# Banded attention rebuilt with float32 operands and a fixed instruction order, ahead of a two-stage feed-forward network

## The chip, the cores and the metric

The kernel runs on one core of a Trainium2 chip. The metric is device time in microseconds (us); lower is better. One profiled execution of the kernel before gives the rows below; its time stands beside its span in the table. PE is the matrix engine (PEld its weight loads), DVE the vector engine, ACT the scalar engine, POOL the general engine GpSimd, SP the engine that issues most transfers.

## The reference

```python
scores = scale * np.matmul(q, k.transpose(0, 1, 3, 2))      # q, k, v: (2, 8, 768, 64)
keep = is_sink | in_window                                  # first 4 positions, or 0 <= rel < 128
a = softmax(np.where(keep, scores, -1e9))
x = np.matmul(a, v)  ->  (1536, 512)
h = x @ w_in;  g = max(h, 0) + log1p(exp(-abs(h)));  x = g @ w_out       # 512 -> 2048 -> 512
h = x @ w_in2; g = h * clip(h + 3, 0, 6) / 6;        out = g @ w_out2    # the same sizes
```

All is float32, with a window of 128 and 4 sinks.

## The kernel before

Sequence positions are cut in groups of 128: `NG` = 12 groups, 6 for each of 2 batch elements. A group of 8 heads is handled as two half groups ("quads") of 4 heads, counted by `n` = 0 to 23 in the main loop of `banded_attention`. A query group needs the keys of its own group and of the one before, and 16 columns for sinks, so a score row has 272 columns (128 in the first group of a batch element, where `i` = 0; sinks are used where `i` > 1).

Every product is made to float32 accuracy out of cheaper ones. Queries and keys are split into a high and a low float32r half by ACT and POOL (L395 to L407), and a score is three matrix products of halves (L456; a head has 64 rows, so the heads of a pair take the two row halves of the array). DVE scales, masks and takes the maximum (L460), ACT takes the exponential (L465), PE transposes the probabilities (L492; the sink columns, gathered by POOL, in L500). ACT and DVE write them out of PSUM as two float16 halves (L475, L478). The values are cut by POOL into three bfloat16 parts (L427, L428), and probabilities times values is five products for each head and block (L533), with three more for the sinks (L517). Then DVE divides by the sum (L541 to L544), PE turns the result (L553), and ACT and DVE store it as two halves of `xT` (L556, L557).

The feed-forward part (`Ffn`) works on blocks of 512 tokens: three blocks of the first network, then three of the second, 16 chunks each; a chunk has 12 products for `h` (L111) and 12 for `y` (L163), 2304 in all. Its weights arrive as 8-byte numbers and each half chunk is converted on the way (`Weights.half`: three DVE steps, L70 to L76, one of ACT, L80, one of POOL, L81). Six such halves are called for inside the attention loop. PE, DVE, ACT and POOL each work through one stream in order; the scheduler of the building program sets that order from the order of the code and its own estimates.

Of the kernel before, what the change touches and what calls it, by code (L numbers as in the profile page):

```python
# [10 lines left out]
F16 = mybir.dt.float16  # L11
# [8 lines left out]
P = 128  # L20
NEG = 1.0e9
PSCALE = 4096.0
# [4 lines left out]
TB = 2  # L27

# [64 lines left out]
class Ffn:  # L93
# [91 lines left out]
    def run(self, specs, out, nblk, w0, pool2):  # L185
# [15 lines left out]
        for s in range(n + 2):  # L201
# [22 lines left out]
def sink_window_attention_ffn_kernel(  # L224
# [46 lines left out]
    with ExitStack() as body:  # L271
# [14 lines left out]
        w.upto(2 * NW0)  # L286
# [4 lines left out]
        for c in range(NW0, 16):  # L291
            for io in range(2):
                w.add("w1", c, io, w1_in, w1_out, wpool1)
        w.fetch()
        ffn.run(specs, out, NT // 512, 2 * NW0, lambda c: wpool0 if c < NW0 else wpool1)
# [3 lines left out]
    with tc.If(rv < 1):  # L299
        nc.scalar.preload_act_table_set("natural_log_exp_and_others")  # L300
        with ExitStack() as body:
# [13 lines left out]
            ffn.run(specs, out, NT // 512, 4, lambda c: wpool)  # L315


def banded_attention(ctx, tc, qT_d, kT_d, v, ident, NSv, Wv, xT, psa, isq, w):
    nc = tc.nc
# [3 lines left out]
    NP = H // 2  # L323

# [6 lines left out]
    st = {}  # L331

    def fetch(g):
        b, i = divmod(g, NB)
        s = st.setdefault(g, {})
        for nm, src in (("q", qT_d), ("k", kT_d)):
            t = two.tile([P, NP, P], F32, tag="n" + nm, bufs=2, name=f"n{nm}_{g}")
            nc.sync.dma_start(t, src[b].rearrange("(p t) d s -> (t d) p s", t=2)[:, :, i * P : (i + 1) * P])
            s["n" + nm] = t
        t = thr.tile([P, H, D], F32, tag="nv", name=f"nv_{g}")  # L340
        nc.sync.dma_start(t, v[b, i * P : (i + 1) * P])
        s["nv"] = t

    def fetch_sinks(b):
        s = st[b * NB]

        t = two.tile([P, H, D], F32, tag="vs", name=f"vs_{b}")
        nc.gpsimd.memset(t, 0.0)
        for r in range(8):
            nc.sync.dma_start(t[r * MAXSINK : (r + 1) * MAXSINK, r % 4 :: 4, :], v[b, 0:MAXSINK, r % 4 :: 4, :])  # L350
        s["nvs"] = t

    fetch(0)


    hid = -NEG / isq
    rmc = one.tile([P, P], F32, name="rmc")
    nc.gpsimd.iota(rmc, pattern=[[-1, P]], base=0, channel_multiplier=1, allow_small_or_imprecise_dtypes=True)
    col = one.tile([P, P], F32, name="col")
    nc.gpsimd.iota(col, pattern=[[1, P]], base=0, channel_multiplier=0, allow_small_or_imprecise_dtypes=True)  # L360
    wm = one.tile([P, 1], F32, name="wm")
    nc.vector.tensor_scalar(out=wm, in0=Wv, scalar1=-float(P), scalar2=None, op0=ALU.add)
# [13 lines left out]
    nc.vector.tensor_tensor(out=m_zero, in0=mB, in1=mS, op=ALU.mult)  # L376
    nc.vector.tensor_tensor(out=m_one[:, 0, 0:P], in0=mA, in1=mS, op=ALU.mult)
    nc.vector.tensor_copy(m_one[:, 1, 0:P], mB)
    nc.vector.memset(m_one[:, :, P:SLOTW], hid)
    nc.vector.tensor_copy(m_odd[:, 0, 0:P], mA)  # L380
    nc.vector.tensor_copy(m_odd[:, 1, 0:P], mB)
    nc.vector.tensor_copy(m_even[:, 0, 0:P], mB)
    nc.vector.tensor_copy(m_even[:, 1, 0:P], mA)
    for m in (m_odd, m_even):
        for j in range(2):
            nc.vector.tensor_scalar(
                out=m[:, j, P:SLOTW], in0=mS[:, j * SK : (j + 1) * SK], scalar1=hid, scalar2=None, op0=ALU.mult
            )

    ring = one.tile([P, 2, NP, 4, SLOTW], F32R, name="ring")  # L390

    def load_q(g):
        s = st[g]
        qT = two.tile([P, 2, NP, P], F32R, tag="qT", bufs=2, name=f"qT_{g}")
        nc.scalar.activation(qT[:, 0], s["nq"], AF.Copy)  # L395
        eng = nc.gpsimd if g else nc.vector
        eng.tensor_tensor(out=qT[:, 1], in0=s["nq"], in1=qT[:, 0].bitcast(F32), op=ALU.subtract)
        s["qT"] = qT

    def load_k(g):  # L400
        b, i = divmod(g, NB)
        s = st[g]
        pos = SLOTPOS[g % 4]
        hi, lo = ring[:, 0, :, pos, 0:P], ring[:, 1, :, pos, 0:P]
        nc.scalar.activation(hi, s["nk"], AF.Copy)  # L405
        eng = nc.gpsimd if g else nc.vector
        eng.tensor_tensor(out=lo, in0=s["nk"], in1=hi.bitcast(F32), op=ALU.subtract)  # L407
        if i == 0:
            ks = two.tile([P, 2, NP, MAXSINK], F32, tag="ks", name=f"ks_{b}")
            for a in range(2):  # L410
                nc.gpsimd.tensor_copy(ks[:, a], ring[:, a, :, pos, 0:MAXSINK].bitcast(F32))
            st["ks", b] = ks
        if i < 4:
            ks = st["ks", b]
            for a in range(2):
                nc.gpsimd.tensor_copy(ring[:, a, :, pos, P:SLOTW], ks[:, a, :, (i % 2) * SK : (i % 2 + 1) * SK])

    def top(x):
        return x.bitcast(BF16).rearrange("p (n t) -> p n t", t=2)[:, :, 1]

    def values(g, src="nv", dst="V", pool=thr):

        s = st[g]
        x = s[src].rearrange("p h d -> p (h d)")
        res = pool.tile([P, H * D], F32, tag=dst + "r", name=f"{dst}r_{g}")
        v3 = pool.tile([P, H * D], BF16, tag=dst + "3", name=f"{dst}3_{g}")
        nc.gpsimd.tensor_tensor(out=res, in0=x, in1=top(x), op=ALU.subtract)  # L427
        nc.gpsimd.tensor_tensor(out=v3, in0=res, in1=top(res), op=ALU.subtract)  # L428
        s[dst] = (top(x), top(res), v3)

    def scores(g, quad):
        b, i = divmod(g, NB)
# [4 lines left out]
        pt = two.tile([P, 4, 2, SLOTW], F32, tag="P", bufs=2, name=f"P_{g}_{quad}")  # L437
        s["P", quad] = pt
        if i == 0:
            mask = m_zero  # L440
            n = P
        else:
            ee, oo = sorted((SLOTPOS[(g - 1) % 4], SLOTPOS[g % 4]))
            mask = (m_one if i == 1 else m_odd if i % 2 else m_even).rearrange("p a c -> p (a c)")
            n = 2 * SLOTW
        for p in range(quad * 2, quad * 2 + 2):

            pss = [psa.tile([P, 512], F32, tag="s", name=f"s_{g}_{p}_{t}")[:, 0:n] for t in range(2)]
            for m, (a, c) in enumerate(((0, 0), (0, 1), (1, 0))):
                for t in range(2):  # L450
                    rows = slice(t * D, (t + 1) * D)
                    if i == 0:
                        rhs = ring[rows, c, p, SLOTPOS[g % 4], 0:P]
                    else:
                        rhs = ring[rows, c, p, ee : oo + 1 : oo - ee, :]
                    nc.tensor.matmul(pss[t], s["qT"][rows, a, p, :], rhs, start=(m == 0), stop=(m == 2))  # L456
            for t in range(2):
                h = 2 * p + t
                xs = thr.tile([P, 2 * SLOTW], F32, tag="xs", bufs=4, name=f"xs_{g}_{h}")[:, 0:n]
                st["ttr"] = nc.vector.tensor_tensor_reduce(  # L460
                    out=xs, in0=pss[t], in1=mask, scale=-isq, scalar=3.0e38,
                    op0=ALU.add, op1=ALU.min, accum_out=s["mx"][:, h : h + 1],
                )
                dst = pt[:, h - quad * 4].rearrange("p a c -> p (a c)")[:, 0:n]
                nc.scalar.activation(  # L465
                    dst, xs, AF.Exp, scale=-1.0, bias=s["mx"][:, h : h + 1], accum_out=s["sum"][:, h : h + 1]
                )

        if i > 1:
            s["PS", quad] = two.tile([P, 2, 4, 2, SK], F32, tag="PS", name=f"PS_{g}_{quad}")  # L470
            for a in range(2):
                nc.gpsimd.tensor_copy(s["PS", quad][:, a], pt[:, :, :, P:SLOTW])

    def evac_hi(t, ps):
        nc.scalar.activation(t, ps, AF.Copy, scale=PSCALE)  # L475

# [228 lines left out]
```

## Time and profile before

| | |
|---|---|
| median of 3 runs | 670.83 us (670.52 to 672.7) |
| the profiled execution | 670.09 us, span 668.2 us |
| busy: PE, DVE, ACT, POOL | 644.7, 364.2, 358.4, 274.9 us |
| mean granted clock of PE | 0.996 |
| attention alone on PE | to 129.3 us of the span, its rest mixed with L111 until 145.8 us |

The span runs from the first to the last instruction. A busy PE is not a PE at its peak, since the ends of pipelined products are modelled; starts of neighbouring rows tell its pace.

### The profile page before, as it was taken

The numbers are of one execution on the slowest core, as the hardware profiler recorded it, in microseconds if no ns is written. First come the engines' busy times: TensorE is split into PE (matmuls) and PEld (weight loads), VectorE is DVE, ScalarE is ACT, GpSimd is POOL, SyncE is SP. The second block draws the span as 40 slices with busy tenths as digits, with TensorE's granted clock in tenths as the row PEclk, the third lists the DMA queues.
The fourth block names the chain that finished last, engine by engine and source line by source line (L and its number), as shares of the span: only waits on it lengthen the run. The fifth ranks groups of instructions, "written<-read, shape, count | busy, mean of one in ns | idle before, by whom it ended". The sixth has DMA issues, their size and how long they took to land.

```text
span 668.2 us, 10211 instructions
## 1 busy us (share of the span) xinstructions
PE 644.7 (96%) x3760; PEld 527.3 (79%) x3760; DVE 364.2 (54%) x730; ACT 358.4 (54%) x755; POOL 274.9 (41%) x272
## 2 busy tenths in 40 slices
PE   1999999999999999999999999999999999999996
PEld 0777877887878888888888888888888888888884
DVE  6468899979998233222689899422232222322222
ACT  2668888786878766566867874322222222222221
POOL 6446756468898545444589894100000000000000
PEclk9999999998999999999999999999999999999999
DMA  6832321289100000001465652000010000100001
GB/s 173 271 92 74 113 64 34 87 275 372 41 1 0 1 0 1 0 1 32 153 196 190 209 164 66 2 0 1 0 64 0 1 1 0 64 0 1 1 0 68
DMA packets 38746, 47.01 MB, mean 70 GB/s; under 512 B 2848, under 2 KB 31520, under 8 KB 38688
## 3 DMA queue, kind: packets, MB, share of 16 engines
q1 hardware_dynamic: 38400, 46.28, 21.6%
q8 instruction: 31, 0.51, 0.3%
q14 instruction: 27, 0.22, 0.1%
q10 hardware_dynamic: 288, 0.00, 0.0%
HBM read 43.12 MB, written 3.15 MB: 69 GB/s over the span
## 4 chain that ended last, share of the span: by engine, by line
PE 89%; DVE 3%; ACT 3%; POOL 2%; issue 2%; DMA 1%; SPq 0%; POOLq 0%; ACTq 0%; DVEq 0%
PE y_w L163 37%; PE h_w L111 36%; PE s L456 6%; PE pt L492 4%; PE o L533 4%; DMA nk<-in_k_dram 1%; PE o L517 1%; POOL w_w L81 1%; PE xtr L553 1%; POOL u_w L132 1%; POOL g_w L138 1%; DVE PT L478 0%; ACT P L465 0%; ACT e_w L129 0%; ACT u_w L130 0%
## 5 line engine op out<-in xcount | busy, mean ns | idle before, releaser
L111 PE MATMUL h_w<-xT,w_w 128*128 128x512 f32 x1152 | 282.4, 391 | 1.8 <-POOL w_w L81 1.3
L111 PEld LDWEIGHTS h_w<-xT,w_w 128*128 128x128 f32 x1152 | 216.4, 188 | 47.7 <-POOL w_w L81 1.7
L163 PE MATMUL y_w<-g_w,w_w 128*128 128x512 f32 x576 | 142.2, 390 | 0.1
L163 PE MATMUL y_w<-w_w,g_w 128*128 128x512 f32 x576 | 138.9, 389 | 0.0
L163 PEld LDWEIGHTS y_w<-g_w,w_w 128*128 128x128 f32 x576 | 108.4, 189 | 23.3 <-POOL g_w L138 0.8
L163 PEld LDWEIGHTS y_w<-w_w,g_w 128*128 128x128 f32 x576 | 107.9, 188 | 23.2 <-ACT g_w L143 0.4
L81 POOL TENSOR_TENSOR w_w<-t_w,w_w 128x512 fp32r<-128x512 f32 x64 | 83.9, 1312 | 33.9 <-ACT w_w L80 33.5
L142 DVE SCALAR_TENSOR_TENSOR h_w<-e_w,h_w 128x512 f32<-128x512 f32 x48 | 33.4, 696 | 89.0 <-ACT e_w L140 89.0
L140 ACT ACTIVATE e_w<-h_w 128x512 f32<-128x512 f32 x48 | 28.7, 599 | 96.2 <-PE h_w L111 94.6
L144 DVE SCALAR_TENSOR_TENSOR g_w<-h_w,g_w 128x512 fp32r<-128x512 f32 x48 | 33.2, 691 | 83.6 <-ACT g_w L143 83.6
L143 ACT ACTIVATE g_w<-h_w 128x512 fp32r<-128x512 f32 x48 | 28.7, 598 | 91.0 <-PE y_w L163 90.7
L132 POOL TENSOR_TENSOR u_w<-u_w,e_w 128x512 f32<-128x512 f32 x48 | 62.2, 1295 | 36.4 <-ACT u_w L131 34.4
L138 POOL TENSOR_TENSOR g_w<-e_w,g_w 128x512 fp32r<-128x512 f32 x48 | 62.2, 1296 | 32.8 <-ACT g_w L137 32.6
L456 PE MATMUL s<-ring,qT 64*128 64x272 f32 (+1 forms) x288 | 47.7, 344 | 14.9 <-ACT ring L405 7.6
L135 DVE SCALAR_TENSOR_TENSOR h_w<-h_w,r_w 128x512 f32<-128x512 f32 x48 | 33.4, 696 | 51.8 <-ACT r_w L133 51.8
L465 ACT ACTIVATE P<-xs,mx 128x272 f32<-128x272 f32 (+1 forms) x96 | 47.3, 496 | 15.4 <-DVE mx L460 15.2
L456 PEld LDWEIGHTS s<-ring,qT 64*128 64x128 f32 x288 | 33.9, 212 | 23.2 <-DVE mx L460 8.8
L136 DVE TENSOR_TENSOR e_w<-h_w,u_w 128x512 f32<-128x512 f32 x48 | 33.0, 688 | 28.6 <-POOL u_w L132 28.4
L80 ACT ACTIVATE w_w<-t_w 128x512 fp32r<-128x512 f32 x64 | 40.0, 625 | 13.1 <-DVE t_w L76 12.8
L128 ACT ACTIVATE e_w<-h_w 128x512 f32<-128x512 f32 x48 | 28.4, 592 | 32.6 <-PE h_w L111 23.3
L137 ACT ACTIVATE g_w<-e_w 128x512 fp32r<-128x512 f32 x48 | 30.0, 624 | 28.1 <-DVE e_w L136 19.5
L70 DVE TENSOR_SCALAR m_w<-raw_w 128x512 int32<-128x512 int32 x56 | 38.8, 693 | 8.3 <-DMA raw_w<-in_moe_w_in_dram 3.8
(89 smaller groups left out, 717.1 us busy)
## 6 DMA issues: line engine op xcount, KB each, us to landing
raw_w<-in_moe_w_in_dram SPq DMA_DIRECT2D x32, 512.0 KB, 4.8
raw_w<-in_moe_w_out_dram SPq DMA_DIRECT2D x32, 512.0 KB, 4.5
nq<-in_q_dram SPq DMA_DIRECT2D x12, 256.0 KB, 3.0
nk<-in_k_dram SPq DMA_DIRECT2D x12, 256.0 KB, 3.7
nv<-in_v_dram SPq DMA_DIRECT2D x12, 256.0 KB, 2.9
out_dram<-o SPq DMA_DIRECT2D x12, 256.0 KB, 2.1
vs<-in_v_dram SPq DMA_DIRECT2D x16, 8.0 KB, 3.4
words<-in_n_sink_dram ACTq DMA_DIRECT2D x1, 1.0 KB, 4.0
```

Source lines behind the costliest of these rows:

```text
L70: nc.vector.tensor_scalar(out=m, in0=hi, scalar1=3, scalar2=0x3FFFFFF8, op0=ALU.logical_shift_left, op1=ALU.bitwise_and)
L80: nc.scalar.activation(wt[:, 0, :], t.bitcast(F32), AF.Copy)
L81: nc.gpsimd.tensor_tensor(out=wt[:, 1, :], in0=t.bitcast(F32), in1=wt[:, 0, :].bitcast(F32), op=ALU.subtract)
L111: nc.tensor.matmul(h, wt[:, ws, kk * P : (kk + 1) * P], xT[:, xs, kk, t0 : t0 + 512], start=(n == 0), stop=(n == 11),)
L132: nc.gpsimd.tensor_tensor(out=u, in0=u, in1=e, op=ALU.subtract)
L135: nc.vector.scalar_tensor_tensor(out=h, in0=h, scalar=0.0, in1=r, op0=ALU.max, op1=ALU.add)
L138: nc.gpsimd.tensor_tensor(out=glo, in0=e, in1=ghi.bitcast(F32), op=ALU.subtract)
L142: nc.vector.scalar_tensor_tensor(out=h, in0=e, scalar=6.0, in1=h, op0=ALU.min, op1=ALU.mult)
L144: nc.vector.scalar_tensor_tensor(out=glo, in0=h, scalar=1.0 / 6.0, in1=ghi.bitcast(F32), op0=ALU.mult, op1=ALU.subtract)
L163: ins = nc.tensor.matmul(y, lhsT, rhs, start=(c == 0 and n == 0), stop=(c == 15 and n == 2))
L456: nc.tensor.matmul(pss[t], s["qT"][rows, a, p, :], rhs, start=(m == 0), stop=(m == 2))
L465: nc.scalar.activation(dst, xs, AF.Exp, scale=-1.0, bias=s["mx"][:, h : h + 1], accum_out=s["sum"][:, h : h + 1])
```

## The change

The attention is written anew. The splits are gone: scores (L457 of the changed kernel), transposes (L499) and probabilities times values (L541, sinks L526) take float32 operands as they are. A score is one product instead of three, a head and block one instead of five. Two copies of 512 columns take the transposed probabilities out of PSUM, one by ACT (L514), one by DVE (L512). There are four score banks instead of three. Keys go by DMA straight into the ring, `fetch` runs three groups ahead instead of two, and the first group's transfers are cut in two and shared between SP and ACT. Masks are made one by one, just before the half group that needs them. 22 products of zeros stand at the start of PE's stream, and 6 in each of the first three rounds. Everything inside `in_order` keeps the order of the code on each engine. Five weight halves are converted inside the attention instead of six (and two behind it), and the first network's weights are listed in another order.

```diff
+HALVES = (5, 9, 13, 17, 21)
+WARM = 22
...
-    nc.scalar.dma_start(words[:, 1, :], window.bitcast(I32).partition_broadcast(P))
+    nc.sync.dma_start(words[:, 1, :], window.bitcast(I32).partition_broadcast(P))
...
+        order = [(0, 0)] + [x for c in range(15) for x in ((c + 1, 0), (c, 1))] + [(15, 1)]
...
-        w.upto(2 * NW0)
...
-        ffn.run(specs, out, NT // 512, 2 * NW0, lambda c: wpool0 if c < NW0 else wpool1)
+        ffn.run(specs, out, NT // 512, w.done, lambda c, io: homes[c, io])
...
-            for m, (a, c) in enumerate(((0, 0), (0, 1), (1, 0))):
-                for t in range(2):
-                    nc.tensor.matmul(pss[t], s["qT"][rows, a, p, :], rhs, start=(m == 0), stop=(m == 2))
+                nc.tensor.matmul(ps, s["q"][rows, p, :], rhs, start=True, stop=True)
...
-            evac_hi(t[:, 0], ps)
-            evac_lo(t[:, 1], ps, t[:, 0])
+        if m == 1:
+            nc.vector.tensor_copy(t, ps)
+        else:
+            nc.scalar.activation(t, ps, AF.Copy)
...
+            for k, (o, gg) in enumerate(blocks):
                 nc.tensor.matmul(
-                    s["o"][:, h, :], lh, rh, start=(i <= 1 and m == 0),
-                    stop=(m == len(terms) - 1 and (i <= 1 or hh == 3)),
+                    s["o"][:, h, :], t[:, o : o + P], st[gg]["v"][:, h, :], start=(k == 0 and (i <= 1 or hh == 0)),
+                    stop=(k == len(blocks) - 1 and i <= 1),
                 )
...
+    def keep_busy(n):
+
+        for _ in range(n):
+            nc.tensor.matmul(spare, z[:, 0:P], z, start=True, stop=True)
+
+    with in_order(tc):
+        fetch(0)
...
+        keep_busy(WARM)
+        masks(0)
+        fetch(1)
+        fetch_sinks(0)
+        fetch(2)
+        keep_sinks(0)
+        for n in range(NQ + 3):
...
+            if new:
+                scores(n)
+            if done is not None:
+                normalise(done)
+            if n < 3:
+                keep_busy(6)
+            if old:
+                transposes(n - 1, 1)
+                transposes(n - 1, 2)
+            if new:
+                exps(n, 0)
+            if n >= 4 and n % 2 == 0:
+                store_lo(n // 2 - 2)
+            if old:
+                copies(n - 1, 1)
+                copies(n - 1, 2)
+                apply_v(n - 1, 0)
+            if new:
+                exps(n, 1)
+                transposes(n, 0)
+            if done is not None:
+                turn_x(done)
+            if old:
+                apply_v(n - 1, 1)
+                apply_v(n - 1, 2)
+                if n % 2 == 0:
+                    inverse((n - 1) // 2)
+            if new:
+                copies(n, 0)
+            if done is not None:
+                store_hi(done)
...
+            if n < 3:
+                masks(n + 1)
+            if n in HALVES:
                 w.half()
```

DVE at the start, in the kernel before: from the first mask step to the first score step (`xs`); `mA` to `m_zero` are masks of 128 rows and 128 columns.

```order
L368 TENSOR_SCALAR mB<-rmc,val 128x128
L371 TENSOR_SCALAR mS<-col,val 128x128
...
L377 TENSOR_TENSOR m_one<-mA,mS 128x128
L380 COPY m_odd<-mA 128x128
L383 COPY m_even<-mA 128x128
L376 TENSOR_TENSOR m_zero<-mB,mS 128x128
L378 COPY m_one<-mB 128x128
L381 COPY m_odd<-mB 128x128
L382 COPY m_even<-mB 128x128
L386 TENSOR_SCALAR m_even<-mS 128x8
L460 ISA xs_0_177,mx_167<-s_0_0_169,m_zero 128x128
```

The same place now:

```order
L409 TENSOR_SCALAR mB<-rmc,val 128x128
L291 TENSOR_TENSOR fl<-fl 128x1
L410 TENSOR_TENSOR mB<-mB,tB 128x128
L293 TENSOR_TENSOR near<-fl 128x1
L411 TENSOR_SCALAR mS<-col,val 128x128
L412 TENSOR_TENSOR m_zero<-mB,mS 128x128
L469 ISA xs_0_197,mx_181<-s_0_183,m_zero 128x128
```

Four mask steps stand ahead of the first score step now; those of `m_one`, `m_even` and `m_odd` have moved behind the score steps of half groups 0, 1 and 2.

PE in the middle of the attention, in the kernel before (group 5, second half; `pt` and `pts` are transposes, `o` the attention's result, of which only the first of 40 pieces stands here):

```order
L456 MATMUL s_2_0_1196<-ring,qT_919 128x272 x3
L492 MATMUL pt_1_0_1120<-ident,P_1_973 128x128 x4
L492 MATMUL pt_1_1_1128<-ident,P_1_973 128x128 x4
L500 MATMUL pts_1_1136<-ident,PS_1_1002 128x128
L456 MATMUL s_2_1_1197<-ring,qT_919 128x272 x3
L456 MATMUL s_3_0_1210<-ring,qT_919 128x272 x3
L517 LDWEIGHTS PTS_0_1023
L517 MATMUL o_1144<-vs_245,PTS_0_1023 128x256
...
L533 MATMUL o_1144<-nv_578,PT_0_0_1010 128x64
```

One whole round of the loop now (`n` = 8, group 4, first half):

```order
L457 MATMUL s_0_631<-ring,q_376 128x272
...
L457 MATMUL s_3_637<-ring,q_376 128x272
L499 MATMUL pt_1_639<-ident,P_562 128x128 x4
L490 MATMUL pts_644<-ident,PS_601 64x128
L541 MATMUL o_590<-v_173,PT_0_618 128x64
...
L541 MATMUL o_590<-v_255,PT_0_618 128x64
L499 MATMUL pt_0_669<-ident,P_630 128x128 x4
L541 MATMUL o_590<-v_173,PT_1_653 128x64
...
L541 MATMUL o_590<-v_255,PT_1_653 128x64
L526 MATMUL o_590<-vs_170,PTS_655 128x256
```

The four heads' scores stand together with their row halves alternating, and between them and the transposes that need them lies work of the half group before; `o` has 8 products and one for the sinks.

## Rows read from the trace of the kernel before

**Rows 1.** Windows: each engine's busy time and instructions, PE's granted clock, DMA, GB/s.
```profile
16.70:41.80 25.10, 25.10 (x156) 19.47 (x156) 12.10 (x49) 15.73 (x51) 11.98 (x12) 1.00 0.71 226
41.80:129.30 87.50, 86.31 (x1192) 69.09 (x1190) 79.59 (x252) 74.95 (x230) 51.92 (x78) 1.00 0.22 62
145.80:232.00 86.20, 84.30 (x362) 68.21 (x361) 67.69 (x103) 64.56 (x116) 69.77 (x55) 0.98 0.27 93
```

**Rows 2.** Timeline of PE: start, length, instructions merged, and the releaser.
```profile
16.69 1.54 PE L456 MATMUL s<-ring,qT 64*128 64x128 f32 x9 [7.25 <-DVE mx L460]
...
28.26 1.12 PE L492 MATMUL pt<-ident,P 128*128 128x128 f32 x4
...
39.54 1.05 PE L456 MATMUL s<-ring,qT 64*128 64x272 f32 x3
...
41.80 0.84 PE L553 MATMUL xtr<-ident,x 128*128 128x128 f32 x4
...
69.99 0.65 PE L456 MATMUL s<-ring,qT 64*128 64x272 f32 x6
...
71.11 0.20 PE L533 MATMUL o<-nv,PT 128*128 128x64 bf16 x1
...
72.27 0.19 PE L533 MATMUL o<-Vr,PT 128*128 128x64 bf16 x1
...
72.86 0.64 PE L456 MATMUL s<-ring,qT 64*128 64x272 f32 x3
73.43 0.66 PE L492 MATMUL pt<-ident,P 128*128 128x128 f32 x4
...
129.33 4.80 PE L111 MATMUL h_w<-xT,w_w 128*128 128x512 f32 x20
...
145.76 5.71 PE L163 MATMUL y_w<-g_w,w_w 128*128 128x512 f32 x24
```

**Rows 3.** Timeline of DVE at the start.
```profile
8.44 1.02 DVE L368 TENSOR_SCALAR mB<-rmc,val 128x128 f32<-128x128 f32 x1
...
9.87 0.29 DVE L370 TENSOR_TENSOR mB<-mB,tB 128x128 f32<-128x128 f32 x1
...
12.55 1.28 DVE L380 COPY m_odd<-mA 128x128 f32<-128x128 f32 x1
...
16.35 0.28 DVE L460 CUSTOM_DVE_ANT_0 xs<-s,m_zero 128x128 f32<-128x128 f32 x1
```

**Rows 4.** The chain that ended last: start, length, what.
```profile
1.24 5.66 DMA nk<-in_k_dram
...
651.25 2.72 PE h_w L111 x12
...
662.73 0.69 DVE o L182
```

**Rows 5.** Groups by line: count, busy us, mean ns of one, idle before.
```profile
L456 PEld LDWEIGHTS s<-ring,qT 64*128 64x128 f32 x288 | 33.9, 212 | 23.2 <-DVE mx L460 8.8 <-ACT ring L405 7.6 <-issue 3.6
...
L73 DVE SCALAR_TENSOR_TENSOR m_w<-raw_w,m_w 128x512 int32<-128x512 int32 x56 | 38.8, 692 | 1.2
...
L460 DVE CUSTOM_DVE_ANT_0 xs<-s,m_odd 128x272 f32<-128x272 f32 x32 | 13.2, 431 | 1.4 <-PE s L456 1.3
...
L460 DVE DVE_READ_ACCUMULATOR2_ANT mx<- 128x1 f32 x96 | 7.9, 82 | 0.0
...
L553 PEld LDWEIGHTS xtr<-ident,x 128*128 128x128 f32 x48 | 5.4, 146 | 0.1
...
L541 DVE TENSOR_SCALAR rs<-sum 128x8 f32<-128x8 f32 x12 | 5.2, 437 | 1.1 <-ACT P L465 1.1
...
L182 DVE COPY o<-y_w 128x512 f32<-128x512 f32 x6 | 4.2, 692 | 5.3 <-PE y_w L163 5.3
```

**Rows 6.** Groups by line of ACT.
```profile
L465 ACT ACTIVATE P<-xs,mx 128x272 f32<-128x272 f32 (+1 forms) x96 | 47.3, 496 | 15.4 <-DVE mx L460 15.2
...
L475 ACT ACTIVATE PT<-pt 128x512 f16<-128x512 f32 x44 | 25.9, 588 | 8.9 <-PE pt L492 8.6
```

More of the change, by code (lines that the diff above doesn't have):

```diff
@@ L21 @@
 NEG = 1.0e9
-PSCALE = 4096.0
 MAXSINK = 16
@@ L331, in banded_attention @@
     st = {}
+    ring = one.tile([P, NP, 4, SLOTW], F32, name="ring")
     def fetch(g):
@@ L353, in banded_attention @@
-    fetch(0)
+        s["q"] = thr.tile([P, NP, P], F32, tag="q", name=f"q_{g}")
+        s["v"] = thr.tile([P, H, D], F32, tag="v", bufs=5, name=f"v_{g}")
+        k = ring[:, :, SLOTPOS[g % 4], 0:P]
+        for ps in (slice(0, NP),) if g else (slice(0, NP // 2), slice(NP // 2, NP)):
+            for t, src, eng in ((s["q"], qT_d, nc.sync), (k, kT_d, nc.sync if g else nc.scalar)):
+                src = src[b].rearrange("(p t) d s -> (t d) p s", t=2)[:, ps, i * P : (i + 1) * P]
+                eng.dma_start(t[:, ps], src)
@@ new lines, in fetch, with own_sinks @@
+        nc.sync.dma_start(s["v"], v[b, i * P : (i + 1) * P])
+    def fetch_sinks(b):
+        t = two.tile([NS, H, D], F32, tag="vs", name=f"vs_{b}")
+        rows = v[b, 0:MAXSINK].rearrange("m h d -> m (h d)")
+        rows = bass.AP(rows.tensor, rows.offset, [[0, 4]] + [list(x) for x in rows.ap])
+        nc.sync.dma_start(t.rearrange("p h d -> p (h d)"), rows)
+        st["vs", b] = t
+    def own_sinks(b):
+        t = st["vs", b]
+        nc.gpsimd.tensor_tensor(
+            out=t, in0=t, in1=owner.rearrange("p (h o) -> p h o", o=1).to_broadcast([NS, H, D]), op=ALU.mult
+        )
@@ L375, in banded_attention @@
     m_zero = one.tile([P, P], F32, name="m_zero")
[L376 to L385, printed above, removed]
+    ph = one.tile([NS, 2, 4], I32, name="ph")
@@ L400, in load_k, with keep_sinks @@
-    def load_k(g):
+                out=m[:, :, P:SLOTW], in0=mS[:, 0:MAXSINK].rearrange("p (a c) -> p a c", a=2),
+                scalar1=hid, scalar2=None, op0=ALU.mult,
+            )
+    def keep_sinks(g):
         b, i = divmod(g, NB)
-        s = st[g]
         pos = SLOTPOS[g % 4]
[L404 to L407, printed above, removed]
@@ L408, in load_k @@
         if i == 0:
[L409 to L412, printed above, removed]
+            st["ks", b] = two.tile([P, NP, MAXSINK], F32, tag="ks", name=f"ks_{b}")
+            nc.gpsimd.tensor_copy(st["ks", b], ring[:, :, pos, 0:MAXSINK])
         if i < 4:
-            ks = st["ks", b]
-            for a in range(2):
-                nc.gpsimd.tensor_copy(ring[:, a, :, pos, P:SLOTW], ks[:, a, :, (i % 2) * SK : (i % 2 + 1) * SK])
@@ L418, in top @@
[L418 to L429, printed above, removed]
@@ L431, in scores @@
-    def scores(g, quad):
-        b, i = divmod(g, NB)
+            nc.gpsimd.tensor_copy(ring[:, :, pos, P:SLOTW], st["ks", b][:, :, (i % 2) * SK : (i % 2 + 1) * SK])
+    def scores(n):
+        g, quad = divmod(n, 2)
+        i = g % NB
         s = st[g]
@@ L469, in scores @@
[L469 to L475, printed above, removed]
-    def evac_lo(t, ps, hi):
-        nc.vector.scalar_tensor_tensor(out=t, in0=ps, scalar=PSCALE, in1=hi, op0=ALU.mult, op1=ALU.subtract)
-    def transposes(g, quad):
+        s["P", quad] = two.tile([P, 4, 2, SLOTW], F32, tag="P", bufs=2, name=f"P_{n}")
@@ new lines, in exps @@
+    def exps(n, pair):
+        g, quad = divmod(n, 2)
+        i = g % NB
+        s = st[g]
+        w_ = P if i == 0 else 2 * SLOTW
+        mask = m_zero if i == 0 else (m_one if i == 1 else m_odd if i % 2 else m_even).rearrange("p a c -> p (a c)")
+        for hh in range(2 * pair, 2 * pair + 2):
+            h = quad * 4 + hh
+            xs = thr.tile([P, 2 * SLOTW], F32, tag="xs", bufs=4, name=f"xs_{n}_{hh}")[:, 0:w_]
+            nc.vector.tensor_tensor_reduce(
+                out=xs, in0=s["s", quad][hh], in1=mask, scale=-isq, scalar=3.0e38,
+                op0=ALU.add, op1=ALU.min, accum_out=s["mx"][:, h : h + 1],
+            )
+            dst = s["P", quad][:, hh].rearrange("p a c -> p (a c)")[:, 0:w_]
+            nc.scalar.activation(
+                dst, xs, AF.Exp, scale=-1.0, bias=s["mx"][:, h : h + 1], accum_out=s["sum"][:, h : h + 1]
+            )
+        if i > 1 and pair == 1:
+            s["PS", quad] = two.tile([P, 4, 2, SK], F32, tag="PS", name=f"PS_{n}")
+            nc.gpsimd.tensor_copy(s["PS", quad], s["P", quad][:, :, :, P:SLOTW])
@@ L481, in transposes @@
+    def transposes(n, m):
+        g, quad = divmod(n, 2)
         i = g % NB
@@ new lines, in copies, with apply_v @@
+    def copies(n, m):
+        g, quad = divmod(n, 2)
+        s = st[g]
+        if ("ps", m) not in s:
+            return
+        ps = s.pop(("ps", m))
+        if m == 2:
+            t = two.tile([NS, P], F32, tag="PTS", name=f"PTS_{n}")
+        else:
+            t = two.tile([P, 512], F32, tag=f"PT{m}", name=f"PT_{n}_{m}")
+        if m == 1:
+            nc.vector.tensor_copy(t, ps)
+        else:
+            nc.scalar.activation(t, ps, AF.Copy)
+        s["T", quad, m] = t
+    def apply_v(n, m):
+        g, quad = divmod(n, 2)
@@ L538, in normalise, with inverse @@
+    def inverse(g):
+        s = st[g]
+        s["rs"] = two.tile([P, H], F32, tag="rs", name=f"rs_{g}")
+        nc.vector.tensor_scalar(out=s["rs"], in0=s["sum"], scalar1=1.0e-9, scalar2=None, op0=ALU.add)
+        nc.vector.reciprocal(s["rs"], s["rs"])
     def normalise(g):
         s = st[g]
-        rs = two.tile([P, H], F32, tag="rs", name=f"rs_{g}")
-        nc.vector.tensor_scalar(out=rs, in0=s["sum"], scalar1=1.0e-9, scalar2=PSCALE, op0=ALU.add, op1=ALU.mult)
-        nc.vector.reciprocal(rs, rs)
@@ L557, in store_x @@
-        nc.vector.tensor_tensor(out=xT[:, 1, :, cols], in0=ps, in1=hi.bitcast(F32), op=ALU.subtract)
-    fetch(1)
-    load_q(0)
-    load_k(0)
-    values(0)
-    NQ = 2 * NG
-    for n in range(NQ + 3):
-        g, quad = divmod(n, 2)
-        if n < NQ:
-            scores(g, quad)
-        if 0 <= n - 1 < NQ:
-            transposes(*divmod(n - 1, 2))
-        if n < NQ and g + 1 < NG:
-            if quad == 0:
-                load_q(g + 1)
-            else:
-                load_k(g + 1)
-                values(g + 1)
-                if g % NB == 0:
-                    fetch_sinks(g // NB)
-                    values(g, "nvs", "VS", two)
-                if g + 2 < NG:
-                    fetch(g + 2)
-        if 0 <= n - 2 < NQ:
-            apply_v(*divmod(n - 2, 2))
-            if n % 2 == 1:
-                normalise((n - 2) // 2)
-        if n % 2 == 0 and n >= 4:
-            store_x(n // 2 - 2)
-        if n in (6, 14, 18, 20, 22, 23):
-            with tc.issue_after(st["ttr"].ins):
+        nc.vector.tensor_tensor(
+            out=xT[:, 1, :, cols], in0=st[g]["xtr"], in1=xT[:, 0, :, cols].bitcast(F32), op=ALU.subtract
+        )
```

213 lines of the change are left out of this document (107 added, 106 removed).

## The prediction

> **What bounds the kernel now.** I read the windows first, then the timeline of PE at the seams between the stages, then the groups for the durations. The windows [rows 1] show PE busy for nearly all of each stage from 16.7 us on. Between 41.8 and 129.3 us DVE (79.6 of 87.5 us) and ACT (75.0) are close behind it, so the attention has three engines near their limit, and behind 145.8 us PE alone is left.
>
> The timeline of PE [rows 2] shows what the windows hide. Its first dense row stands at 16.69 us behind 7.25 us of idle time that DVE's `mx` ended; DVE was making masks from 8.44 us to its first score step at 16.35, some steps in 0.3 us and some of the same size in 1.0 to 1.3 [rows 3]. Then the same row has two paces: four transposes take 1.12 us at 28.26 and 0.66 at 73.43; three score products take 1.05 us at 39.54 and 0.64 at 72.86. The row at 41.80 stands at the change. The column of the granted clock reads 1.00 throughout [rows 1], but by these durations PE ran at the lower of its two levels (1.2 GHz) until 41.8 us and at 2.4 GHz from there.
>
> Balance: twelve `h` products take 2.72 us [rows 4], 0.227 each, so 2304 of them 522.3 us. When the attention's last piece ends at 145.76, 48 products of `h` (four rows like the one at 129.33) have been done in between [rows 2], 10.9 us, so the attention with its start costs 134.9 us. Of the other 533.3 us, 522.3 are products, 5.5 lie behind the last step at 662.73 [rows 4], and 5.5 are stalls. Half group 4 begins about where the first `xtr` stands, 41.8; 20 half groups in 93.1 us are 4.65 us each.
>
> **The change part by part.** *Start.* Four mask steps of about 0.3 us come ahead of the first score step, and POOL's splits, beside which DVE's mask steps were slow, are gone. The first keys landed at 6.9 us [rows 4] and go straight into the ring now; half of them is enough to begin. The 22 products of zeros are 5.0 us at the pace of `h`, 10 at half of it, from about 1 us on; they lie in the wait for data. I put the first scores at 9 us (bounds 7 and 11), against 16.7. The window's transfer moves ahead of the queries on SP, 0.5 us, and the keys go to ACT's queue behind one other transfer: no matter at this length. Behind them on SP stand the groups' and the weights' transfers, 23 us ahead of their use at three groups; a slot of the ring is free when the scores two groups back are done.
>
> *Float32 products.* The trace has none, except transposes. Bounds: a transpose's weight load is 5.4/48 = 0.113 us of PEld [rows 5], and a streamed column is 2.72/12/512 = 0.44 ns [rows 4]. At the least, a float32 product is one load and one stream, like a transpose; at the most, four of each, since each operand has a high and a low half, as the old splits show. I take two loads (two halves of the stationary side) and four streams. That is nearest to what the old code does by hand, which has two loads of different weights among its three products. A piece of probabilities times values, 64 columns, is then two loads, 0.225 us (streams 0.11 hidden), bounds 0.113 and 0.45; before, 40 pieces went from 71.11 to 72.27, 0.03 each [rows 2], 1.2 us for a half group. Now 8 × 0.225 = 1.8. A score of 272 columns is 4 × 0.12 = 0.48 us. Six score products at 69.99 took as long as three at 72.86 [rows 2]: alternating row halves run side by side. So four heads take 0.96 us, bounds 0.5 and 1.93. The sink product, 256 columns, is 0.45.
>
> *One round of a half group with sinks* on PE: scores 0.96, nine transposes at 0.113 and half of four more 1.24, pieces 1.8, sinks 0.45, two changes between 64 and 128 rows 0.2 (three streams of 0.12 at 72.86 fill 0.57 us up to the next row, so 0.1 to 0.2 each): 4.65 us. On DVE: four score steps at 0.43 + 0.08 [rows 5] 2.05, one copy 0.69, and by halves the low store 0.69, the division 0.69 and the two inverse steps 0.63, 1.0: 3.75. On ACT: exponentials 47.3/96 with what their sums add, 0.6 × 4 [rows 6], copies 0.59 and 0.27, half a store: 3.6. PE bounds. In its fixed order the transposes of pair 0 come 2.5 us behind the start of the scores; the first two heads reach them after 0.5 + 0.2 + 2 × 0.51 + 0.7 = 2.4 us. It just fits, and I add nothing. A half group with `i` = 0 is set by DVE, 3.2; with `i` = 1, without sinks, 4.0.
>
> *Weights.* Each `half` puts 3 × 0.69 us [rows 5] at the end of a round on DVE. Queued behind them are the next round's score steps, and behind those the exponentials and pair 0's transposes. DVE has 0.9 us of slack in a round, some of it earlier: I take 0.4 us for each of five, 2 us. POOL's part (1.3 us) stands ahead of the next copy of sink columns, needed a round later. Three conversions more fall into the first block: DVE 67.7 + 6.2 of 86.2 us there, POOL 69.8 + 3.9, ACT 64.6 + 1.9 [rows 1]: still covered by PE. If not, 1.3 us each on POOL, 4 us in all. The fourth score bank and the deeper fetch take away waits that rows 1 leave 1.2 us for, so nothing.
>
> *Sum.* Start 9. Half groups 0 to 3: with one round in flight, latency sets them, four score steps, a copy, a round of masks and the exponential to transpose path, 4 us each: 16, at the upper clock, against 25.1. Half groups 4 to 23: 16 × 4.65 + 2 × 3.2 + 2 × 4.0 + 2 = 90.8, against 93.1. Attention 115.8, against 134.9: 19.1 us less. Nothing else moves: span 668.2 - 19.1 = 649, and with the 1.9 us between span and time **651 us**. The profiled execution, 670.09, lies 0.7 below the median, so against the median it is the same within what matters. In short: the pace of the middle stays as it is, and the gain is the start and the clock.
>
> **The rivals.** *Four loads.* If each of the four streams loads its own weights, a piece costs 0.45: 176 pieces × 0.225 = 40 us more, 691 us, slower. It decides from 0.34 us a piece (0.225 + 20/176). For it: a pass with half weights could not keep them; against: the stationary side has two halves only. The Trainium skill (FP8 and Floating Point Precision, TensorE Precision Notes) counts four passes through the array for true float32; it does not say how many loads, and no row here has one. Chance 0.10.
>
> *Heads in a row, not side by side.* The old overlap came from three short products a head. If a float32 head must end before the next one begins, each round takes 0.96 us more, 20 rounds with 272 columns 19 us: 670, no change. With an overlap of the seam alone (a head's second half beside the next head's first, 5 steps instead of 4), 0.24 a round, 5 us: 656. The Trainium skill (TensorE: Matmul & The Clock Gate, Part 3) says that matmuls start and end strictly in program order, which would give the seam alone. The rows at 69.99 alternate already, so they don't decide. 0.10 for the full loss; the seam lies in my range.
>
> *The clock, or the order.* If PE falls back to its lower level while rounds 0 to 3 trickle, or rises late as it did before, they take 25 us as before: 660. For it: PE was dense for 25 us at the lower level [rows 1, 2] before it rose, with the same kinds of work before and behind; against: the 22 products of 512 columns come first now, and nothing of that size stood there. A fixed order that fits so closely can cost about 0.5 us a round, 10 us, too: 661. Together 0.20.
>
> *Cheaper products.* One load for a piece takes 0.9 us from each round; then DVE, 4.1 us in the rounds with a store, bounds: 0.5 us for 16 rounds, 8 us: 643. With the start at 7 us, 641. 0.12.
>
> **How the numbers follow.** Forecast 651 (643 to 658 by the start's bounds and the seam) 0.48, cheaper 0.12, clock or order 0.20, heads in a row 0.10, four loads 0.10. What this kernel's measurement can tell from no change is 0.3%, 2 us. Forecast, cheaper, clock and order are faster, with a fifth of heads in a row: 0.82. Same: 0.05. Slower: four loads and the rest, 0.13. The range reaches from the cheaper case with an early start, 635, to heads in a row, 672; it leaves out four loads and the far ends.
>
> **What would show it.** Right: first scores near 9 us; transposes four in 0.6 us from the start; starts of `o` pieces 0.22 apart; four heads in about 1 us; rounds of 4.65 us with PE waiting little; `h` first at about 107 us; behind it the old pace. Wrong: two or four weight loads at a piece's place that take 0.45; PE idle before `pt` for DVE or ACT; transposes in 1.1 us behind 9 us; new waits for `w_w` in the first block. The prediction falls if a float32 piece costs over 0.34 us.

## The result and the profile after

The changed kernel takes **659.22 us** (median of 4 runs, 658.93 to 659.35) against 670.91 in the same runs: ratio 0.982, interval 0.9802 to 0.9838. It is faster by 1.8%, 11.7 us. The forecast was 651 us: the sign was right, and 8 us of the gain are missing. The profiled execution has a span of 657.5 us. Of the run with three score banks below, one of six executions (708.75 us, at a lower clock) is left out of the median and the ratio.

The windows, in the columns of [rows 1]: from the first scores to half group 4, from there to the last half group's scores, the rest of the attention, and the 20 us behind it.

```profile
8.58:24.10 15.52, 14.39 (x107) 10.39 (x106) 9.32 (x48) 8.62 (x34) 1.40 (x4) 1.00 0.95 281
24.10:108.00 83.90, 82.09 (x661) 71.26 (x660) 63.05 (x225) 59.23 (x197) 13.09 (x26) 1.00 0.34 100
108.00:126.00 18.00, 17.82 (x105) 14.26 (x104) 5.87 (x16) 4.82 (x16) 0.48 (x2) 1.00 0.02 5
126.00:146.00 20.00, 11.80 (x41) 9.62 (x42) 18.94 (x29) 16.80 (x31) 14.75 (x12) 0.74 1.04 365
```

The first three windows are full. In the last, PE works for 11.8 of 20 us at a mean granted clock of 0.74, while DVE and ACT, which had been idle for most of the 18 us before, are full. The timeline of PE, whose counterpart is [rows 2], shows where:

```profile
1.19 7.46 PE L577 MATMUL spare<-z 128*128 128x512 bf16 x22 [1.19 <-DVE z L582]
8.58 0.72 PE L457 MATMUL s<-ring,q 64*128 64x128 f32 x8
...
12.58 0.60 PE L499 MATMUL pt<-ident,P 128*128 128x128 f32 x4
...
22.29 0.61 PE L499 MATMUL pt<-ident,P 128*128 128x128 f32 x4
22.73 0.60 PE L563 MATMUL xtr<-ident,x 128*128 128x128 f32 x4
23.17 1.00 PE L541 MATMUL o<-v,PT 128*128 128x64 f32 x8
24.10 1.19 PE L457 MATMUL s<-ring,q 64*128 64x272 f32 x8
25.22 0.66 PE L499 MATMUL pt<-ident,P 128*128 128x128 f32 x4
25.71 1.00 PE L541 MATMUL o<-v,PT 128*128 128x64 f32 x8
26.55 0.61 PE L499 MATMUL pt<-ident,P 128*128 128x128 f32 x4
...
103.97 1.27 PE L457 MATMUL s<-ring,q 64*128 64x272 f32 x7
...
108.03 0.48 PE L526 MATMUL o<-vs,PTS 64*128 64x256 f32 x1
108.04 0.49 PE L457 MATMUL s<-ring,q 64*128 64x272 f32 x1
...
108.37 1.26 PE L457 MATMUL s<-ring,q 64*128 64x272 f32 x7
...
125.29 0.66 PE L563 MATMUL xtr<-ident,x 128*128 128x128 f32 x4
134.20 5.43 PE L136 MATMUL h_w<-xT,w_w 128*128 128x512 f32 x12 [8.26 <-ACT w_w L105]
```

Read starts against starts (`pt` and `xtr` are transposes of the probabilities and of the attention's result). Four transposes take 0.44 us (22.29 to 22.73), four pieces of probabilities times values, two records each, 0.84 (25.71 to 26.55), the four heads' scores 1.12 (24.10 to 25.22). Then comes what the forecast did not have, at the seam between the attention and the feed-forward part: PE stands idle for 8.26 us, and the next twelve `h` products take 5.43 us instead of 2.72, the lower of the two clock levels. ACT's timeline at that place:

```profile
118.12 0.27 ACT L514 ACTIVATE PTS<-pts 64x128 f32<-64x128 f32 x1 [2.14 <-PE pts L490]
125.98 0.60 ACT L566 ACTIVATE xT<-xtr 128x512 fp32r<-128x512 f32 x1 [7.59 <-PE xtr L563]
126.48 1.08 ACT L153 ACTIVATE e_w<-h_w 128x512 f32<-128x512 f32 x2
```

PE did 36 products of `h` (three chunks) between 111 and 125 us, so the first chunk, `h_0`, was ready at some 114.4 us, 12 us before its first step on ACT (L153), which stands in ACT's order behind the attention's last store of `xT`. The three banks of `h` stay full until DVE's L161, some steps later, has read `h_0`, and the fourth chunk has no place. In the kernel before, four chunks of `h` were done by the end of the attention [rows 2]. The profile names the converted weights (`w_w`) as what ended the wait; POOL's and DVE's timelines say otherwise:

```profile
129.19 1.28 POOL L106 TENSOR_TENSOR w_w<-t_w,w_w 128x512 fp32r<-128x512 f32 x1 [16.43 <-ACT w_w L105]
...
133.37 0.69 DVE L161 TENSOR_TENSOR e_w<-h_w,u_w 128x512 f32<-128x512 f32 x1
```

The first weight half finished behind the attention, the sixth, which `h_3` needs, is there at 130.5 us; L161 ends at 134.1, and PE goes on at 134.20.

### The profile page after: what moved, and what is told of

It is laid out like the page before. It is cut to its first block, busy times and chain, and to the rows that moved or that the text cites. A ratio compares the mean times of both kernels' runs of the same rounds, so it can differ in the third digit from the quotient of the medians.

```text
span 657.5 us, 8828 instructions
## 1 busy us (share of the span) xinstructions
PE 639.1 (97%) x3160; PEld 525.9 (80%) x3160; DVE 336.9 (51%) x693; ACT 333.5 (51%) x707; POOL 214.2 (33%) x197
## 4 chain that ended last, share of the span: by engine, by line
PE 94%; DVE 2%; issue 1%; ACT 1%; POOL 0%; DVEq 0%; ACTq 0%; POOLq 0%
PE h_w L136 40%; PE y_w L188 40%; PE o L541 5%; PE s L457 3%; PE pt L499 3%; PE spare L577 2%; PE o L526 1%; PE xtr L563 1%; DVE xs L469 0%; DVE PT L512 0%; ACT P L474 0%; DVE xT L570 0%; POOL ring L434 0%; PE pts L490 0%; ACT w_w L105 0%
## 5 line engine op out<-in xcount | busy, mean ns | idle before, releaser
L153 ACT ACTIVATE e_w<-h_w 128x512 f32<-128x512 f32 x48 | 28.3, 592 | 39.3 <-PE h_w L136 30.1
L541 PE MATMUL o<-v,PT 128*128 128x64 f32 x352 | 45.1, 271 | 2.0 <-DVE PT L512 2.0
L161 DVE TENSOR_TENSOR e_w<-h_w,u_w 128x512 f32<-128x512 f32 x48 | 33.0, 687 | 25.2 <-POOL u_w L157 25.2
L541 PEld LDWEIGHTS o<-v,PT 128*128 128x128 f32 x352 | 42.8, 191 | 3.3 <-DVE PT L512 2.8
L95 DVE TENSOR_SCALAR m_w<-raw_w 128x512 int32<-128x512 int32 x59 | 40.9, 693 | 8.3 <-DMA raw_w<-in_moe_w_in_dram 3.6
L101 DVE SCALAR_TENSOR_TENSOR t_w<-raw_w,m_w 128x512 int32<-128x512 int32 x59 | 40.3, 683 | 3.5 <-POOL g_w L163 0.5
```

Source lines behind the costliest of these rows:

```text
L95: nc.vector.tensor_scalar(out=m, in0=hi, scalar1=3, scalar2=0x3FFFFFF8, op0=ALU.logical_shift_left, op1=ALU.bitwise_and)
L101: nc.vector.scalar_tensor_tensor(out=t, in0=lo, scalar=29, in1=m, op0=ALU.logical_shift_right, op1=ALU.bitwise_or)
L541: nc.tensor.matmul(s["o"][:, h, :], t[:, o : o + P], st[gg]["v"][:, h, :], start=(k == 0 and (i <= 1 or hh == 0)), stop=(k == len(blocks) ...
```

## The experiments

**At the seam.** Theory A was that queue: the scratch memory of the feed-forward steps is allocated behind the attention and shares its memory, so the scheduler puts their first steps behind the attention's last ones. Theory B was what the profile names, the converted weights (`w_w`): five halves are made inside the attention now, and `h_3` needs the sixth.

```diff
-HALVES = (5, 9, 13, 17, 21)
+HALVES = (5, 7, 9, 11, 13, 16, 19, 21)
```

> Changed kernel, with eight weight halves converted inside the attention instead of five (after half groups 5, 7, 9, 11, 13, 16, 19, 21); the scratch memory of the first h steps still stands in memory that the attention used. In the changed kernel PE stands idle 8.3 us ahead of h_3 (134.2 us) and then runs 10 us at the lower clock. Theory A (the queue: ACT and DVE can't begin the work on h_0 before the attention's last stores, so the score banks come free late): the wait stays at 5 us or more, and the time at 655 to 659 us. Theory B (the late weight half w_3_0, the sixth): the wait falls under 2 us, and the time comes to 649 to 652 us.

Measured: 659.02 us, ratio to the kernel before 0.9835 (0.982 to 0.9849), no gain. The weights were there, PE waited all the same, and its timeline now names DVE's L161, the step that frees a bank:

```profile
133.98 5.39 PE L136 MATMUL h_w<-xT,w_w 128*128 128x512 f32 x12 [7.57 <-DVE e_w L161]
```

```diff
+        ffn.tmp = body.enter_context(tc.tile_pool(name="tmp", bufs=1))
         with ExitStack() as att:
             banded_attention(att, tc, qT, kT, v, ident, NSv, Wv, xT, psa, ISQ, w)
-        ffn.tmp = body.enter_context(tc.tile_pool(name="tmp", bufs=1, reuse_waits="tile"))
```

> Changed kernel, with the scratch pool of the feed-forward steps allocated ahead of the attention, so that it shares no memory with it; five halves as before. The Abs of h_0 then stands ahead of the last two stores of xT in ACT's order. Theory A (the queue): the idle time ahead of h_3 falls under 3 us, 648 to 652 us. Theory B (the weight half alone): the idle time stays near 8 us, 657 to 660 us. Both: 4 to 5 us of idle time stay, some 653 us.

Measured: 653.51 us, ratio 0.9752 (0.9739 to 0.9765). ACT takes `h_0` 13 us earlier, ahead of the last two stores; what is left on PE is two short waits, and behind them thirteen products at the lower level (0.45 us each):

```profile
113.49 0.60 ACT L153 ACTIVATE e_w<-h_w 128x512 f32<-128x512 f32 x1 [0.27 <-PE h_w L136]
```

```profile
124.75 0.65 PE L563 MATMUL xtr<-ident,x 128*128 128x128 f32 x4 [0.79 <-DVE x L555]
...
128.46 5.83 PE L188 MATMUL y_w<-g_w,w_w 128*128 128x512 f32 x13 [2.35 <-DVE xT L570]
```

Both edits together:

> Both edits at once: eight halves inside the attention, and scratch memory of its own for the feed-forward steps. Either theory, and their mixture: no wait of over 2 us at the seam, the upper clock kept, 648 to 650 us. If it stays above 655 us, neither the queue nor the weight half is the cause. Against the first two kernels it tells how far the two add.

Measured: 650.69 us, ratio 0.9708 (0.9695 to 0.9721). PE is busy throughout at the upper level:

```profile
110.00:130.00 20.00, 20.00 (x113) 16.61 (x113) 8.46 (x20) 14.11 (x31) 6.62 (x6) 1.00 0.51 158
```

So A was the main cause, 5.7 us alone; the weight half is the next in line, worth nothing alone and 2.8 us once the queue is gone.

**The zeros, the clock and the order.** The changed kernel without its products of zeros:

```diff
-        keep_busy(WARM)
...
-            if n < 3:
-                keep_busy(6)
```

> Changed kernel without the products of zeros (22 at the start, 6 in each of the first three rounds). If they are what holds the upper clock in the first rounds (the forecast's step): transposes four in 1.1 us until about 30 to 35 us, half groups 0 to 3 in 22 to 25 us instead of 15.5, the time some 6 to 9 us more, 665 to 668 us. If the rounds are bound by latency on DVE and ACT, or the float32 products raise the clock themselves: under 2 us more, 657 to 661 us.

Measured: 658.07 us, ratio 0.9826 (0.981 to 0.9843): the zeros are worth nothing.

```profile
7.29 2.77 PE L457 MATMUL s<-ring,q 64*128 64x128 f32 x16 [7.29 <-DMA ring<-in_k_dram]
9.99 1.11 PE L499 MATMUL pt<-ident,P 128*128 128x128 f32 x4
...
15.90 1.97 PE L499 MATMUL pt<-ident,P 128*128 128x128 f32 x8
...
18.83 1.19 PE L457 MATMUL s<-ring,q 64*128 64x272 f32 x8
19.95 0.66 PE L499 MATMUL pt<-ident,P 128*128 128x128 f32 x4
...
23.10 1.19 PE L457 MATMUL s<-ring,q 64*128 64x272 f32 x8
```

The scores start 1.3 us earlier, when the keys land; PE is at its lower level (four transposes in about 1 us) until the row at 15.90, and at the upper one by 18.83. Yet half groups 0 to 3 take 15.8 us, against 15.5 with the zeros. The zeros cost there about what the clock brings: two sets of 6 stand in PE's queue ahead of the first transposes, which come 4.0 us behind the first scores with them (8.58 to 12.58) and 2.7 without (7.29 to 9.99), and the faster products behind have that back. How long these rounds would take at the upper clock without zeros in the queue, no run shows.

The same question put to the kernel before:

```diff
+    z = one.tile([P, 512], BF16, name="z")
+    nc.vector.memset(z, 0.0)
+    spare = ps1.tile([P, 512], F32, tag="tr", bufs=2, name="spare")
+    for _ in range(56):
+        nc.tensor.matmul(spare, z[:, 0:P], z, start=True, stop=True)
```

> Kernel before, with 56 products of zeros (128x512) at the start of PE's stream, which end about where its second row of scores stands (16.7 us); nothing else changed. It tells how much of the forecast's 9 us in half groups 0 to 3 is the clock alone. If it is the clock: four transposes in 0.6 us from the start, these half groups in 16 to 17 us instead of 25, the time 8 us less, 661 to 663 us. If they are bound by other things, or if the old products let the clock fall again: under 2 us less, 668 to 671 us.

Measured: 670.57 us, ratio 0.999 (0.9975 to 1.0006). The timeline, and the window that answers to the first of [rows 1]:

```profile
16.99 0.97 PE L460 MATMUL s<-ring,qT 64*128 64x128 f32 x9 [0.84 <-DVE mx L464]
19.99 0.77 PE L496 MATMUL pt<-ident,P 128*128 128x128 f32 x2 [2.03 <-POOL Vr L431]
```

```profile
16.70:41.80 25.10, 22.78 (x170) 17.79 (x170) 12.10 (x56) 15.90 (x51) 12.73 (x14) 0.59 0.74 233
```

The clock was up (nine scores in 0.97 us instead of 1.54 at 16.69 before), fell after the idle 2.03 us, and the mean over the window is 0.59. So zeros ahead of that loop don't keep the clock, and nothing is won. The scheduler also set another order behind them, so this run doesn't price the clock alone.

Then the changed kernel with its order set by the scheduler:

```diff
-    with in_order(tc):
+    with ExitStack():
```

> Changed kernel without the fixed order inside the attention: the building program's scheduler sets the order on each engine, as in the kernel before; all else is as in the changed kernel. If the order written by hand carries the pace of the middle: PE idle before pt or o in each round, 0.3 to 1 us each, 6 to 20 us more, 665 to 680 us. If the work on PE alone sets the pace: within 3 us, 656 to 662 us. The wait at the seam may move either way, and is read by itself.

Measured: 678.85 us, ratio 1.0143 (1.0103 to 1.0183): slower than the kernel before, 19.6 us more than with the fixed order.

```profile
9.18 0.72 PE L457 MATMUL s<-ring,q 64*128 64x128 f32 x8
...
15.27 0.33 PE L499 MATMUL pt<-ident,P 128*128 128x128 f32 x1
18.02 2.18 PE L457 MATMUL s<-ring,q 64*128 64x272 f32 x6 [2.42 <-DVE mx L469]
...
29.16 1.06 PE L499 MATMUL pt<-ident,P 128*128 128x128 f32 x4
...
34.73 0.61 PE L563 MATMUL xtr<-ident,x 128*128 128x128 f32 x4
```

PE stood idle for 2.42 us, fell to the lower level although the zeros had come first, and stayed there past 30 us. The first `xtr` comes at 34.73 instead of 22.73, 12 us late; 6.4 more are lost by the end of the attention, and the wait at the seam is the same (8.25 us). From the first scores (9.18) to that `xtr` it takes 25.6 us, about as long as in the kernel before (16.69 to 41.80, [rows 2]), so without the fixed order the gain in the fill, half groups 0 to 3, is gone. How much of the 12 us is the order itself, and how much the clock that fell in its gap, this run doesn't separate.

> Changed kernel, with all masks made ahead of the first score step, as before the change, instead of just before the half group that needs them: eight more DVE steps there, six of them 0.28 us, about 2 us in all. If the forecast's start term holds (each mask step ahead of the first score step delays the end): first score step at about 10 to 11 us instead of 9.1, 1 to 2 us more, 660 to 661 us. If the rounds give it back, since they are rid of the mask steps: within 0.5 us, 659 us.

This run makes the masks up front (a loop over `masks(i)` ahead of the rounds). Measured: 658.96 us, ratio 0.9843 (0.981 to 0.9875), no difference. On DVE the first of the added steps and the first score step:

```profile
8.16 0.35 DVE L415 TENSOR_SCALAR mA<-rmc,wm 128x128 f32<-128x128 f32 x1
...
9.60 0.28 DVE L469 CUSTOM_DVE_ANT_0 xs<-s,m_zero 128x128 f32<-128x128 f32 x1
```

Half group 4 begins 0.45 us later, and the profiled execution's span is 0.5 longer (658.0 us), too little for the medians to tell; that the rounds, rid of the masks, give it back isn't shown. The steps that took 1.0 to 1.3 us [rows 3] take 0.2 to 0.35 at the same place, with POOL busy for 1.85 of the 8 us from 8 to 16. That POOL had slowed them fits, but no run tests it alone.

**The fourth bank.**

```diff
-                ps = (psa if hh < 3 else ps1).tile([P, 512], F32, tag="s" if hh < 3 else "s3", ...)
+                ps = psa.tile([P, 512], F32, tag="s", ...)
```

> Changed kernel, with three score banks instead of four: the fourth head's scores wait until DVE has taken the first head's. The forecast gave the fourth bank nothing: 657 to 660 us. The rival: in a fixed order everything on PE queues behind that wait; the first score step ends some 0.5 us after the first head's scores, of which the other two heads hide 0.5, so 0.2 to 0.5 us of idle time ahead of the fourth head in each of 24 rounds, 5 to 12 us more, 664 to 671 us.

Measured: 683.42 us, ratio 1.0228 (1.0186 to 1.0271), 24 us more, twice the most that the rival gave. PE and DVE in two rounds, the second with a division (L555) on DVE:

```profile
48.39 1.27 PE L457 MATMUL s<-ring,q 64*128 64x272 f32 x5
49.85 0.72 PE L457 MATMUL s<-ring,q 64*128 64x272 f32 x2 [0.19 <-DVE mx L469]
...
53.67 1.26 PE L457 MATMUL s<-ring,q 64*128 64x272 f32 x5
55.16 0.72 PE L457 MATMUL s<-ring,q 64*128 64x272 f32 x2 [0.22 <-DVE mx L469]
...
59.41 1.27 PE L457 MATMUL s<-ring,q 64*128 64x272 f32 x5
```

```profile
49.34 0.44 DVE L469 CUSTOM_DVE_ANT_0 xs<-s,m_even 128x272 f32<-128x272 f32 x1 [2.46 <-PE s L457]
...
54.05 0.69 DVE L555 TENSOR_TENSOR x<-o,rs 128x512 f32<-128x512 f32 x1 [1.13 <-PE s L457]
54.66 0.43 DVE L469 CUSTOM_DVE_ANT_0 xs<-s,m_even 128x272 f32<-128x272 f32 x1
```

In the first round DVE waits for the first head's scores (2.46 us idle), its score step ends at 49.8, and PE, with everything queued behind the fourth head, starts that at 49.85. In the second the division stands ahead of the score step, the first bank is free at 55.1, and the fourth head starts at 55.16. It is 1.5 us behind the row of the other heads both times, so the division is not what costs. The first round takes 5.28 us (48.39 to 53.67), the second 5.74 (53.67 to 59.41), against 4.4 and 4.8 with four banks. The idle times of 0.19 and 0.22 in the rows hide most of that, since ends are modelled; and the fourth head runs alone, some 0.65 us (55.16 to the transposes at 55.81), instead of beside another.

**Heads side by side.** The four heads in the order 0, 2, 1, 3 (`for t in range(2)` outside of the loop over `p`, with masks of sinks and heads to match):

> Changed kernel, with the four heads' scores in the order 0, 2, 1, 3, so that two heads with the same row half of the array follow each other twice; pairs, masks and sinks follow that order, the sums are the same. Side by side (the forecast's step): heads of the same half can't overlap, two of the three seams become 0.2 to 0.5 us longer, a round some 0.5 to 0.9 us, 20 rounds 10 to 18 us more, 669 to 677 us. In a row (the rival: a float32 score is short by itself, and its place doesn't matter): under 0.1 us a round, 658 to 661 us.

Measured: 660.49 us, ratio 0.9846 (0.9827 to 0.9865); the four heads take 1.12 us as before (starts at 73.23 and 74.35). That could mean either of two things, so every head was put on one half:

```diff
-                rows = slice(t * D, (t + 1) * D)
+                rows = slice(0, D)
```

> Changed kernel, with every head's scores computed from the first row half (the odd heads take the even heads' rows, so their scores are not those asked for; the number and size of all instructions stay). The run with the order 0, 2, 1, 3 moved nothing (660.5 us), which either means that heads don't run side by side, or that PE takes the head of the other half from behind a waiting one. In a row already: no change, 658 to 661 us. Side by side (the forecast's step, four streams of 0.12 us a head): four heads take 1.9 to 2.2 us instead of 1.1, 0.8 to 1.1 us more in each of 20 rounds and half of that in 4, 675 to 683 us.

Measured: 677.33 us, ratio 1.011 (1.009 to 1.0131), 18 us more.

```profile
53.60 1.99 PE L457 MATMUL s<-ring,q 64*128 64x272 f32 x8
55.52 0.66 PE L499 MATMUL pt<-ident,P 128*128 128x128 f32 x4
```

Four heads take 1.92 us, 0.48 each, the forecast's four streams of 0.12. So heads do run side by side. In the order 0, 2, 1, 3 strict turns would leave only the middle two together, 0.48 more a round or some 9 us; the medians differ by 1.3 us, and the intervals overlap. In the trace the eight records of that round start in four pairs, 0.01 us apart within a pair (73.23 and 73.24, 73.56 and 73.57, 73.79 and 73.80, 74.02 and 74.03). Score records of one half start 0.23 us apart in the run with one half, so the two of a pair lie on different halves: PE began head 1, on the other half, ahead of head 2, which was queued before it.

**The best version:** eight halves, own scratch memory, no zeros.

> The version with eight halves and scratch memory of its own, without any products of zeros. Without the zeros alone the first scores came 1.3 us earlier (7.29 us instead of 8.58) and half group 4 began 1.0 us earlier (23.10 instead of 24.10). If that carries to the end: 649.3 to 650 us, against 650.7. If the seam needs the zeros for nothing but its place changes with the start: 650 to 652 us.

Measured: **650.10 us**, ratio 0.9692 (0.9678 to 0.9707). It beats both kernels; against the run with zeros (650.69) the intervals overlap.

## Why the prediction was right in sign and 8 us off

By its own terms, from the rows above:

| | forecast | measured |
|---|---|---|
| first scores | 9 | 8.6 |
| half groups 0 to 3 | 16 | 15.5 |
| half group 4 to the end, less `h` | 90.8 | 93.5 |
| attention | 115.8 | 117.6 |
| the rest | 533.3 | 539.9 |
| span | 649 | 657.5 |

(The attention ends at 125.73, with the last transpose's place; 36 `h` products are 8.16 us.)

*The prices of float32 products* held. A piece costs 0.21 (0.225), a transpose 0.11 (0.113), four heads 1.12 (0.96), so *four loads* and *cheaper products* are out; *heads in a row* is out by the run with one half, and the overlap of the seam alone by the four pairs. On the four streams, the Trainium skill (FP8 and Floating Point Precision, TensorE Precision Notes) agrees: it counts four passes, and a head alone takes 0.48 us, four times 272 columns.

*The middle* was 2.7 us off, by two errors. The 19 rounds from 24.10 to 108.04 took 83.9 us, 2.2 less than forecast: those with sinks alternate between 4.4 and 4.8, and the weight halves cost less than 0.4 (three more of them moved the first `h` by 0.5 us in all). But behind the last scores the attention still needed 9.5 us of PE, not one round of 4.65: the drain, two half groups' pieces and the last transposes, was left out.

*Start and fill* had the right sizes, in part by luck. "The gain is the start and the clock" stands in part at most. The zeros don't "lie in the wait for data": 22 take 7.46 us and hold the scores back by 1.3, and in the rounds they cost about what the upper clock brings. Masks just in time bring nothing that can be measured. What the runs show in its place is the fixed order: in it the clock rises by itself (by 18.83 us without zeros), and without it the clock falls in spite of the zeros and the first `xtr` comes 12 us later. How much of the 9.6 us won in half groups 0 to 3 is the clock, and how much the shorter work in its order, stays open. The reading of [rows 1, 2] that PE was "dense for 25 us at the lower level" before was too quick, since merged rows with modelled ends look denser than they are; the run with zeros shows gaps of 0.84 and 2.03 us in that loop. What kept the clock down for so long there stays open.

*The fourth bank* at "nothing" was wrong as a price, though not in the sum: the row of waits belonged to the old order. In the new one it is worth 24 us.

*The step that failed* is **"Nothing else moves"**, with its neighbour "still covered by PE. If not, 1.3 us each on POOL, 4 us in all". The rest grew by 6.6 us: the forecast had carried over 5.5 us of old stalls, and now there are about 12, of which 11 lie at the seam, 8.26 us of PE's idle time and 2.7 on twelve products at the lower level. The forecast had looked for a new wait at the weights, and listed `w_w` among the signs; the profile even names `w_w`. But the weights alone change nothing, own scratch memory brings 5.7 us, both 8.5 (5.5 and 8.3 against the run with eight halves alone, measured together with both). That version lands at 650.7, on the forecast, but by two errors that cancel: its attention is 2 us longer than forecast and its rest 2 us shorter. The 11 us at the seam are not all won back: the version with both edits has waits of its own behind (1.3 us, its profile below) and an attention 0.3 us longer; 0.8 us I leave unassigned.

```profile
PE y_w L188 <- POOL g_w L163: 1.3, 3, 0.6
```

That shared memory is what holds the steps back is shown by the edit that gives them memory of their own; that the scheduler's rule for shared memory does it is argued.

## What to carry to other kernels

Where a stage is rebuilt, look at its last 15 us on every engine, not only on the bound one: what do the next stage's first steps stand behind, and whose memory and banks do they need? A price for a buffer, read from waits in the old order, says nothing of the new order; in the fixed order here one bank more decided 24 us. Judge how dense an engine is by starts of neighbouring rows, and test a warm-up by taking it away.

## What the runs showed of the hardware

- A float32 product stands as two records in the trace, each with its own weight load: 0.11 us apart at 64 columns. On 64 rows a record of 272 columns takes 0.23 us (the run with one half), and records on the two row halves run together; the sink product and a score start 0.01 us apart at 108.03.
- Program order does not hold between the halves (the runs with another order and with one half). The Trainium skill (TensorE: Matmul & The Clock Gate, Part 2, Step-by-step) says that products stay in program order and only weight loads are pulled ahead; these runs speak against it for products on different row halves. What stands ahead of the prediction, that PE works through one stream in order, holds with that exception.
- The clock fell after 2.03 us of idle time (kernel before with zeros), after 2.42 (scheduler's order) and after 8.26 (the seam), each time with dense work ahead of the gap; it rose in the run without zeros while PE did nothing but float32 products with gaps under 1 us. The granted clock reads 1.00 in windows at the start (as in [rows 1], of which only the last window has less, 0.98) where durations show the lower level.
